# A block product without sums taken second, in a bank of its own, in the last two tiles of an attention + GELU feed-forward kernel

## The chip, the cores and the metric

The kernel runs on one NeuronCore of a Trainium2 chip. The metric is the device time of one execution in microseconds. A core has five engines with instruction queues of their own, each worked off in order: TensorE (PE in the profile, its weight loads PEld), VectorE (DVE), ScalarE (ACT), GpSimd (POOL) and SyncE (SP), which here only issues DMAs. TensorE writes to PSUM, a memory of eight banks that hold 512 fp32 numbers in each of 128 partitions; VectorE and ScalarE read the results from there.

## The reference

Sliding-window attention over 8 batches and 8 heads (576 positions, 64 channels, a window of 32 to each side), followed by a feed-forward layer on all 4608 tokens:

```python
scores = (q @ k^T) / 8, masked to |i - j| <= 32
attn   = softmax(scores);  o = attn @ v
x = o.transpose(0, 2, 1, 3).reshape(4608, 512)
h = x @ w_in                                            # 512 -> 2048
g = 0.5 * h * (1 + tanh(sqrt(2/pi) * (h + 0.044715 * h**3)))
out = g @ w_out                                         # 2048 -> 512, fp32
```

All inputs and the output are fp32; the kernel multiplies in fp16 and sums in fp32.

## The kernel before

The 4608 tokens are worked on in nine tiles of 512 (t = 0 to 8). One pass of the main loop (line 911) brings the feed-forward of tile t and, woven into it, the attention of a later batch. ffn_in makes the transposed hidden values in PSUM, gelu (on ScalarE) puts them into the fp16 tile gT, and ffn_out multiplies them with w_out16.

From tile 1 on the second layer is a Winograd-Strassen product of 2x2 blocks: seven block products in place of eight. gT is cut into blocks A11, A12, A21, A22 (halves of the hidden columns and of the tokens), w_out16 into B11 to B22, and VectorE makes sums of the gelus, S1 to S4 (sums, line 672, instructions of L680), as these come. T1 to T4 are differences of the weights, made once. The table WINO (line 41) names the seven products in the order in which they are taken, each with a flag that says whether it begins a new sum in its bank:

| n | product | bank | what is read from the bank after it |
|---|---|---|---|
| 0 | A11*B11 | pys[0], new | M1 = copy (ScalarE in tiles 7 and 8, L748), kept where C21 will be |
| 1 | S2*T2 | pys[1], new | U2 = bank + M1 (L750), kept in C12 |
| 2 | A12*B21 | pys[0], on top of n = 0 | C11 = copy (L752) |
| 3 | S3*T3 | pys[1], on top of n = 1 | U3 = bank + M1 (L757), kept in C22 |
| 4 | S1*T1 | pys[0], new | C22 = bank + U3 (L760; in tile 8 two halves, L763) |
| 5 | A22*T4 | pys[1], on top of n = 3 | C21 = bank + M1 (L766), then stores of rows 2 and 3 |
| 6 | S4*B22 | pys[0], on top of n = 4 | C12 = bank + U2 in two halves (ffn_last, L775), then stores of rows 0 and 1 |

"Rows" are the four groups of 128 tokens of a tile, held in yo. Each product is 16 matmuls of 128x128 weights and 256 columns: eight hidden blocks f for each of two token groups blk. The loop index i runs over the 112 matmuls, so n = i // 16. In the last two tiles product 1 takes six blocks f of both token groups first and the last two of both afterwards. Matmuls and evacuations are put into the queues in this order; a dependence between engines becomes a semaphore wait on the later instruction. A product that goes on in a bank can start only when what was read from the bank before has been read.

In tiles 7 and 8 the first layer is a Winograd product too. in_mixed (line 618) goes through the list MIX (line 62), an order of products, copies, gelus and sums written by hand. It ends `g14 15 gA01 gB01 t1 t2 g15 t3 u1 u2 u3`: gelus of plain columns (L643) and of combined ones (L639), and the sums S1, S2 (t) and S3, S4 (u) of gelu columns 1 to 3.

In tile 7 the pass of ffn_out also holds the end of the last batch's attention: at i = 40 its value products (v-1, L481 and L491), at i = 66 the division (x-1, L532), and at i = 84 in_x (line 592, L600), four VectorE subtractions that prepare tile 8's first layer. Tile 8 has nothing beside its products. Its second token group in n = 4 and n = 6 goes to a bank of its own (pys["apart"], tile py in the profile), so that C22 and C12 can be read in halves. Tile 7 stores through GpSimd's queue (four or five DMAs a store of two rows), tile 8 through SyncE's and ScalarE's (L697 and L699).

psS holds two tiles of two banks, with the tags S0 and S1. In tiles 7 and 8 S1 is used by in_mixed for the third product of the first layer (pu2) and is then unused until the next tile.

Of the kernel before, what the change touches and what calls it, by code (L numbers as in the profile page):

```python
# [9 lines left out]
FP32 = mybir.dt.float32  # L10
FP16 = mybir.dt.float16
AF = mybir.ActivationFunctionType
ALU = mybir.AluOpType
# [23 lines left out]
def cut(b):  # L37
    return 120 if b else 128
# [23 lines left out]
MIX = ("3 g3 A0 s0A B0 s0B A2 B2 cA00 cB00 A1 s1A A4 B1 s1B gA00 gB00 B4 t0 u0 12 A3 s3A B3 s3B g12 cA11 cB11 13 "  # L62
       "A5 B5 gA11 gB11 g13 14 gA10 gB10 A6 B6 cA01 cB01 g14 15 gA01 gB01 t1 t2 g15 t3 u1 u2 u3").split()
UNITS = {"A": 1, "B": 2}

PLAN_1 = {12: "s0@0 s1@1 s2", 16: "m0 m1", 36: "m2", 45: "v0@1 v1 s-1@0", 52: "x0", 55: "x1", 62: "m-1",
          69: "s3@0 v2 v-1@1", 73: "m3", 81: "x2", 85: "x-1", 91: "v3 s4@1", 112: "x3 m4"}
# [11 lines left out]
def kernel(  # L79
# [9 lines left out]
    nc = tc.nc  # L89
# [5 lines left out]
    NT = NTOK // 512  # L95
# [22 lines left out]
    psS = ctx.enter_context(tc.tile_pool(name="psS", bufs=1, space=PSUM))  # L118
# [229 lines left out]
    def bank(i):  # L348

        return psM.tile([128, 512], FP32, name="mm", tag=f"x{i}")  # L350
# [158 lines left out]
    def size(b, g):  # L509
        return 4 * cut(b) if g < 4 else 4 * NPAIR * (144 - cut(b))  # L510
# [66 lines left out]
    def in_w(eng, unit, *which):  # L577

        i = UNITS[unit]
        A11, A12, A21, A22 = (w_in16[:, d:d + 2, c + 256 * i:c + 256 * i + 256] for c in (0, 1024) for d in (0, 2))  # L580
# [21 lines left out]
    def in_product(unit, n):  # L602
        a, w, new = WINO[n]
        if n == 0:
            phs[unit, "a"] = psO.tile([128, 512], FP32, name="pu", tag="O") if unit == "A" else bank(1)
        elif n in (2, 4):
            which = "b" if n == 2 else "c"
            if unit == "A":
                phs[which] = psS.tile([128, 2, 512], FP32, name="pu2", tag="S1" if n == 2 else "S0")
            phs[unit, which] = phs[which][:, "AB".index(unit), :]  # L610
        ps = phs[unit, "b" if n == 2 else "c" if n in (4, 6) else "a"]
        lhs, rhs = mixed[unit, "w"][a], mixed["x"][w]
        for h in range(2):
            for d in range(2):
                nc.tensor.matmul(ps[:, 256 * h:256 * h + 256], lhs[:, d, 128 * h:128 * h + 128], rhs[:, d, :],  # L615
                                 start=(n in (0, 2, 4) and h == d == 0), stop=(h == d == 1), skip_group_check=True)

    def in_mixed(t):
# [5 lines left out]
        for step in MIX:  # L624
            kind, rest = step[0], step[1:]
            if kind in UNITS:
                in_product(kind, int(rest))
# [4 lines left out]
            elif kind == "c":  # L632
                x, which = place[rest[1:]]
                x = mixed[rest[0]][:, x, :]
                nc.vector.tensor_tensor(x, phs[rest[0], which], x, op=ALU.add)
            elif kind == "g" and rest[0] in UNITS:
                r, c, j = int(rest[1]), int(rest[2]), UNITS[rest[0]]
                src = phs[rest[0], "a"] if rest[1:] == "10" else mixed[rest[0]][:, place[rest[1:]][0], :]
# [44 lines left out]
    pys = {}  # L683

    def store(t, t4, yo, cols=slice(0, 512), *engs):

        m = i = 0
        while m < 128:
            b, c = divmod(t * 512 + t4 * 128 + m, S)
            q0, n = (0, cut(b)) if c < 4 * cut(b) else (cut(b), 144 - cut(b))  # L690
            j, p = divmod(c - 4 * q0, n)
            e = min(n - p, 128 - m)
            nj = 1 if p else max(1, min(4 - j, (128 - m) // n))
            eng = engs[i % len(engs)] if engs else nc.gpsimd
            if nj > 1:
                e = nj * n
                eng.dma_start(out_v[b, j:j + nj, q0:q0 + n, cols], yo[m:m + e, cols])  # L697
            else:
                eng.dma_start(out_v[b, j, q0 + p:q0 + p + e, cols], yo[m:m + e, cols])  # L699
            m += e  # L700
            i += 1
# [16 lines left out]
    def ffn_out(t, i):  # L718

        n, blk, f = i // 16, i // 8 % 2, i % 8  # L720
        if n == 1 and t >= NT - 2:
            blk, f = divmod(i % 16, 6) if i % 16 < 12 else (i // 2 % 2, 6 + i % 2)
        a, w, new = WINO[n]
        end = t == NT - 1
        if i % 16 == 0 and new:
            pys[n % 2] = bank((1 + n) % 2)
            if end and n == 4:
                pys["apart"] = psO.tile([128, 512], FP32, name="py2", tag="O")
        py = pys[n % 2].rearrange("p (b c) -> p b c", b=2)
        apart = end and blk and n in (4, 6)  # L730
        if a[0] == "A":
            r0, c0 = 8 * (int(a[2]) - 1) + f, 256 * (int(a[1]) - 1) + 128 * blk
            lhsT = gTs[t][:, r0, c0:c0 + 128]
        else:
            lhsT = wino[a][:, f, 128 * blk:128 * blk + 128]
        one = end and n in (4, 6)
        nc.tensor.matmul(pys["apart"][:, 0:256] if apart else py[:, blk, :], lhsT,  # L737
                         wino[w][:, f, :], start=(new and i % (8 if one else 16) == 0),
                         stop=(i % (8 if one else 16) == (7 if one else 15)),
                         skip_group_check=True)  # L740
        if i % 16 < 15:
            return
        yo, left, right = wino["yo"], slice(0, 256), slice(256, 512)
        C11, C12, C21, C22 = (yo[:, r:r + 2, c] for r in (0, 2) for c in (left, right))

        M1, U2, U3 = C21, C12, C22
        if n == 0:
            (nc.scalar.copy if t >= NT - 2 else nc.vector.tensor_copy)(M1, py)  # L748
        elif n == 1:
            nc.vector.tensor_tensor(U2, py, M1, op=ALU.add)  # L750
        elif n == 2:
            nc.vector.tensor_copy(C11, py)  # L752
            if end:
                for x in range(2):
                    store(t, x, yo[:, x, :], left, nc.sync)
        elif n == 3:
            nc.vector.tensor_tensor(U3, py, M1, op=ALU.add)  # L757
        elif n == 4:
            if not end:
                nc.vector.tensor_tensor(C22, py, U3, op=ALU.add)  # L760
            else:
                for x, part in enumerate((py[:, 0, :], pys["apart"][:, 0:256])):
                    nc.vector.tensor_tensor(C22[:, x, :], part, U3[:, x, :], op=ALU.add)  # L763
                    store(t, 2 + x, yo[:, 2 + x, :], right, nc.sync, nc.scalar)
        elif n == 5:
            nc.vector.tensor_tensor(C21, py, M1, op=ALU.add)  # L766
            for x in range(2):
                store(t, 2 + x, yo[:, 2 + x, :], *((left, nc.sync, nc.scalar) if end else ()))

    def ffn_last(t):  # L770
        py = pys[0].rearrange("p (b c) -> p b c", b=2)
# [139 lines left out]
    for t in range(NT):  # L911
        b = t + 1
# [37 lines left out]
        for i in range(113 if t else 65):  # L950
# [5 lines left out]
            for act in plan.get(i, "").split():  # L956
# [18 lines left out]
                elif kind in "np":  # L975
# [7 lines left out]
                    if kind == "n":  # L983
                        n = size(1, g)
# [45 lines left out]
            if t == 0 and i < 64:  # L1030
                ffn_out_0(*ORDER_0[i])
            elif t and i < 112:
                ffn_out(t, i)
# [36 lines left out]
```

## Time and profile before

| | |
|---|---|
| time, median of 5 runs | 302.72 us (301.56 to 305.35) |
| the profiled execution's own time | 303.57 us |
| its span, first to last instruction | 301.9 us |
| mean granted TensorE clock | 0.999 |
| TensorE busy | 286.7 us, 95% of the span |
| VectorE, ScalarE, GpSimd busy | 212.3, 195.2, 99.6 us |
| tile 7's second layer: first matmul of n = 0, first of n = 6 | 257.45 us, 269.04 us |
| tile 8's second layer: first matmul of n = 0, first of n = 6 | 283.96 us, 295.32 us |
| last addition of tile 8 | 297.26 to 297.68 us |

The page of the profile gives busy times, waits and chains of waits by source line. Lines of the instructions in order of time read: start in us, length in us, engine, source line, operation, output <- input (a buffer's name without its number), partitions x columns and type, how often, and in brackets the idle time of that engine just before and what ended it. In the names mm is a bank of pys or of the first layer, s one of the sums S1 to S4, t one of T1 to T4, w_out one of the blocks B, y the output tile yo, and xc the values of in_x. A matmul's length includes the time in which its last results drain, so the distance between the starts is what it costs in a stream.

### The profile page before, as it was taken

The page shows a single profiled execution, that of the slowest core. Times are in us where ns is not written, and L with a number is a line of the kernel's source. Part 1 is how long each engine was busy: PE and PEld are TensorE (multiplying, and loading weights), DVE is VectorE, ACT ScalarE, POOL GpSimd, SP SyncE. Part 2 cuts the span into 40 slices and gives each one's busy share as a digit, 9 for nine tenths or more (in the row PEclk, how much of TensorE's full clock was granted, in tenths as well). Part 3 has the DMA queues.
Part 4 walks back from the last instruction along what each step waited for, and adds up shares of the span by engine and source line. Part 5 has one row for each costly group of instructions (what it writes and reads, how often), then busy time and mean ns, then how long its engine had stood idle before and what let it go on. Part 6 is the DMA issues. An engine that isn't in the chain of part 4 may idle for free.

```text
span 301.9 us, 7286 instructions
## 1 busy us (share of the span) xinstructions
PE 286.7 (95%) x2941; PEld 183.8 (61%) x2941; DVE 212.3 (70%) x467; ACT 195.2 (65%) x313; POOL 99.6 (33%) x149
## 2 busy tenths in 40 slices
PE   7899899899999799999999799999999999999993
PEld 2534444446774488458845685478647867786683
DVE  4752577897975875868586968766896677865772
ACT  4866667679667676578657846686668656715700
POOL 3435425302843070507280906050720070015000
PEclk9999999999999999999999999999999999999999
DMA  7999998999999999898998995989691031004013
GB/s 216 269 294 383 355 289 235 251 198 180 238 186 186 173 247 208 154 144 215 171 198 125 244 141 127 138 211 177 119 192 31 2 82 62 2 3 137 1 39 103
DMA packets 115944, 50.76 MB, mean 168 GB/s; under 512 B 97495, under 2 KB 109399, under 8 KB 115910
## 3 DMA queue, kind: packets, MB, share of 16 engines
q1 hardware_dynamic: 86756, 37.62, 60.3%
q0 software_dynamic: 28032, 11.62, 26.6%
q10 hardware_dynamic: 1122, 1.06, 1.1%
q8 instruction: 23, 0.38, 0.6%
q14 instruction: 11, 0.09, 0.1%
HBM read 36.70 MB, written 9.44 MB: 153 GB/s over the span
## 4 chain that ended last, share of the span: by engine, by line
PE 60%; DMA 19%; SPq 7%; ACT 5%; DVE 5%; issue 2%; POOL 0%; DVEq 0%; ACTq 0%
PE mm L737 26%; PE mm L563 12%; PE ph L563 12%; DMA wst<-in_moe_w_in_dram 5%; DMA kr<-in_k_dram 4%; DMA tr<-in_q_dram 4%; DMA KT<-k 3%; PE ps_s L454 2%; PE pu L615 2%; PE ps_d L481 2%; DMA wst<-in_moe_w_out_dram 2%; DVE s L680 2%; SPq L182 2%; ACT gT L639 2%; DMA tr<-in_k_dram 2%
## 5 line engine op out<-in xcount | busy, mean ns | idle before, releaser
L563 PEld LDWEIGHTS <-w_in 128*128 128x128 f16 x512 | 49.6, 98 | 57.2 <-DVE w_in L228 0.8
L563 PE MATMUL ph<-xT,w_in 128*128 128x512 f16 x256 | 64.1, 379 | 0.2 <-POOL w_in L853 0.2
L563 PE MATMUL mm<-xT,w_in 128*128 128x512 f16 x256 | 63.7, 379 | 0.0
L571 ACT ACTIVATE gT<-mm 128x512 f16<-128x512 f32 x60 | 35.6, 597 | 33.3 <-PE mm L563 32.7
L737 PEld LDWEIGHTS <-s 128*128 128x128 f16 x512 | 49.4, 98 | 7.6 <-issue 0.9
L699 POOL DMA_DIRECT2D out_dram<-y x55 | 32.4, 597 | 59.4 <-DVE y L766 45.6
L737 PE MATMUL mm<-t,s 128*128 128x256 f16 x376 | 45.0, 273 | 0.6 <-DVE y L750 0.2
L737 PEld LDWEIGHTS <-gT 128*128 128x128 f16 x384 | 36.0, 98 | 6.9 <-issue 0.5
L467 ACT ACTIVATE pe<-ps_s 128x960 f16<-128x960 f32 (+1 forms) x31 | 29.5, 975 | 15.8 <-PE ps_s L454 15.7
L571 ACT ACTIVATE gT<-ph 128x512 f16<-128x512 f32 x58 | 32.2, 600 | 11.1 <-PE ph L563 11.1
L680 DVE TENSOR_TENSOR s<-gT 128x512 f16<-128x512 f16 x64 | 26.7, 418 | 15.6 <-ACT gT L571 14.5
L737 PE MATMUL mm<-w_out,gT 128*128 128x256 f16 x256 | 32.8, 273 | 0.0
L104 ACT ACT_TABLE_LOAD x18 | 23.1, 1283 | 2.2 <-issue 1.9
L516 ACT ACTIVATE lt<-ps_d 128x480 f32<-128x480 f32 (+2 forms) x28 | 15.6, 556 | 11.3 <-PE ps_d L481 7.7
L517 ACT ACTIVATE lt<-lt 128x480 f32<-128x480 f32 (+3 forms) x36 | 21.1, 586 | 1.1
L476 DVE TENSOR_TENSOR pe<-pe,band 128x960 f16<-128x960 f16 x28 | 20.8, 758 | 1.1 <-ACT pe L467 0.9
L194 POOL DMA_DIRECT2D V<-in_v_dram x20 | 17.9, 909 | 1.4 <-issue 1.4
L491 PEld LDWEIGHTS <-V 128*64 128x64 f16 x520 | 13.9, 111 | 6.4 <-DVE V L204 1.5
L737 PE MATMUL mm<-t,gT 128*128 128x256 f16 x128 | 16.3, 273 | 0.0
L680 DVE TENSOR_TENSOR s<-s,gT 128x512 f16<-128x512 f16 x32 | 15.2, 474 | 1.1
L454 PE MATMUL ps_s<-QT,KT 64*64 64x128 f16 (+3 forms) x576 | 13.5, 216 | 2.5 <-DMA KT<-k 1.8
L454 PEld LDWEIGHTS <-KT 64*64 64x64 f16 x576 | 10.0, 106 | 8.6 <-issue 3.8
(148 smaller groups left out, 396.6 us busy)
## 6 DMA issues: line engine op xcount, KB each, us to landing
kr<-in_k_dram SPq DMA_DIRECT2D x31, 256.0 KB, 11.1
qr<-in_q_dram SPq DMA_DIRECT2D x6, 1024.0 KB
wst<-in_moe_w_in_dram SPq DMA_DIRECT2D x7, 512.0 KB, 8.1
V<-in_v_dram POOLq DMA_DIRECT2D x20, 128.0 KB, 8.6
wst<-in_moe_w_out_dram SPq DMA_DIRECT2D x2, 1024.0 KB
wst<-in_moe_w_out_dram SPq DMA_DIRECT2D x4, 512.0 KB
qr<-in_q_dram SPq DMA_DIRECT2D x7, 256.0 KB, 8.3
out_dram<-y POOLq DMA_DIRECT2D x6, 192.0 KB, 5.8
```

Of the source, the lines that this page charges most:

```text
L104: nc.scalar.add_instruction(mybir.InstLoadActFuncSet(name=nc.get_next_instruction_name(), act_func_set_id=which, ins=[], outs=[]))
L194: nc.gpsimd.dma_start(V[:, c, :, :], v[b, :, 128 * c:128 * c + 128, :].rearrange("h p d -> p h d"))
L454: nc.tensor.matmul(sides[h][64 * half:64 * half + 64, 4 * n * r:4 * n * r + 4 * n].rearrange("k (j p) -> k j p", j=4)[:, :, p0 - q0:p1 - q ...
L467: nc.scalar.activation(pe, ps[:, :, 0:w], AF.Exp, scale=SCALE)
L476: nc.vector.tensor_tensor(pe, pe, m.rearrange("k (o j) p -> k o j p", o=1).broadcast_to(list(pe.shape)), op=ALU.mult)
L516: nc.scalar.activation(lt[:, 0:n], d[:, 0:n], AF.Ln)
L517: nc.scalar.activation(lt[:, 0:n], lt[:, 0:n], AF.Exp, scale=-1.0)
L563: nc.tensor.matmul(ph, w_in16[:, dc, fc * 128:fc * 128 + 128], xT[:, dc, t * 512 % RING:t * 512 % RING + 512], start=(dc == 0), stop=(dc = ...
L571: nc.scalar.activation(gTs[t][:, fc, :], phs[fc], AF.Gelu_apprx_tanh)
L680: nc.vector.tensor_tensor(dst, x, y, op=op)
L699: eng.dma_start(out_v[b, j, q0 + p:q0 + p + e, cols], yo[m:m + e, cols])
L737: nc.tensor.matmul(pys["apart"][:, 0:256] if apart else py[:, blk, :], lhsT, wino[w][:, f, :], start=(new and i % (8 if one else 16) == 0) ...
```

## The change

In tiles 7 and 8 the seven products are taken in the order 0, 5, 1, 2, 3, 4, 6. Product 5 (A22*T4), which needs no sums of gelus, comes second. It begins a sum of its own in the first bank of S1 (py5) instead of going on in pys[1]. C21 is then this bank plus U3, added by VectorE right behind U3 and thus behind product 3. U3 holds the other two products of C21 and M1, so the value is the same. The stores of rows 2 and 3 follow C22 in tile 7; in tile 8 the left columns are stored behind C21 and the right columns behind C22. Product 1 takes its blocks in the plain order, all of one token group and then all of the other. Tiles 1 to 6 are as before.

```diff
+ORDER = [0, 5, 1, 2, 3, 4, 6]
...
     def ffn_out(t, i):
 
         n, blk, f = i // 16, i // 8 % 2, i % 8
-        if n == 1 and t >= NT - 2:
-            blk, f = divmod(i % 16, 6) if i % 16 < 12 else (i // 2 % 2, 6 + i % 2)
+        late = t >= NT - 2
+        if late:
+            n = ORDER[n]
         a, w, new = WINO[n]
         end = t == NT - 1
-        if i % 16 == 0 and new:
+        if late and n == 5:
+            new = True
+            if i % 16 == 0:
+                pys["apart5"] = psS.tile([128, 2, 512], FP32, name="py5", tag="S1")[:, 0, :]
+        elif i % 16 == 0 and new:
             pys[n % 2] = bank((1 + n) % 2)
             if end and n == 4:
                 pys["apart"] = psO.tile([128, 512], FP32, name="py2", tag="O")
-        py = pys[n % 2].rearrange("p (b c) -> p b c", b=2)
+        py, py5 = (pys[x].rearrange("p (b c) -> p b c", b=2) if x in pys else None
+                   for x in ("apart5" if late and n == 5 else n % 2, "apart5"))
         apart = end and blk and n in (4, 6)
...
         elif n == 3:
             nc.vector.tensor_tensor(U3, py, M1, op=ALU.add)
+            if late:
+                nc.vector.tensor_tensor(C21, py5, U3, op=ALU.add)
+                if end:
+                    for x in range(2):
+                        store(t, 2 + x, yo[:, 2 + x, :], left, nc.sync, nc.scalar)
         elif n == 4:
             if not end:
                 nc.vector.tensor_tensor(C22, py, U3, op=ALU.add)
+                if late:
+                    for x in range(2):
+                        store(t, 2 + x, yo[:, 2 + x, :])
             else:
                 for x, part in enumerate((py[:, 0, :], pys["apart"][:, 0:256])):
                     nc.vector.tensor_tensor(C22[:, x, :], part, U3[:, x, :], op=ALU.add)
                     store(t, 2 + x, yo[:, 2 + x, :], right, nc.sync, nc.scalar)
-        elif n == 5:
+        elif n == 5 and not late:
             nc.vector.tensor_tensor(C21, py, M1, op=ALU.add)
             for x in range(2):
-                store(t, 2 + x, yo[:, 2 + x, :], *((left, nc.sync, nc.scalar) if end else ()))
+                store(t, 2 + x, yo[:, 2 + x, :])
```

## The prediction

> **What bounds the kernel now.** I read the page first, for the bounding engine, then the chain of work that ended last from 250 us on, and then the instructions in order of time, engine by engine, in tiles 7 and 8, the only ones that the change touches. The page:
>
> ```profile
> span 301.9 us, 7286 instructions
> PE 286.7 (95%) x2941; PEld 183.8 (61%) x2941; DVE 212.3 (70%) x467; ACT 195.2 (65%) x313; POOL 99.6 (33%) x149
> ```
>
> TensorE is the bound overall. In late tiles, the little time that it doesn't work is what the change can win. The chain shows where the end hangs on something else (start, length, what):
>
> ```profile
> 259.69 0.43 DVE s L680
> 260.12 0.05 issue
> 260.17 2.36 PE mm L737 x20
> ...
> 289.42 0.61 DVE y L750
> 290.04 0.04 issue
> 290.08 2.78 PE mm L737 x24
> ```
>
> In tile 7 the second product (S2*T2) is held by VectorE's sums of gelus (L680). In tile 8 the fourth is held by the add L750, which itself stands behind the sums in VectorE's queue. Tile 7 in order of time:
>
> ```profile
> 257.45 1.91 PE L737 MATMUL mm<-w_out,gT 128*128 128x256 f16 x16
> 258.79 0.62 ACT L643 ACTIVATE gT<-mm 128x512 f16<-128x512 f32 x1
> 259.46 2.19 PE L737 MATMUL mm<-t,s 128*128 128x256 f16 x16
> 260.17 1.21 PEld L737 LDWEIGHTS <-s 128*128 128x128 f16 x12 [0.39 <-DVE s L680]
> ```
>
> The 32 unbroken matmuls from 263.80 to the next product at 267.29 give 109 ns each, **1.745 us a product** (a group's length adds the last one's drain). So product 0 leaves TensorE free at 259.20. Product 1 starts at 259.46: its bank is the last plain gelu's, read until 258.79+0.62 = 259.41. Four matmuls later (259.90) it waits for the sums until 260.17. **Two holes, 0.26 + 0.27 = 0.53 us.** Tile 8 has the same two (start 285.97, then 286.68), and a third, 0.34 us: product 2 ends at 288.00+1.745 = 289.74, product 3 starts at 290.08. There is no such hole in tile 7, where attention matmuls take 0.55 us in product 2 (262.36 to 262.91).
>
> What VectorE has to do at the end of tile 7:
>
> ```profile
> 265.74 0.69 DVE L757 TENSOR_TENSOR y<-mm,y 128x512 f32<-128x512 f32 x1 [1.05 <-PE mm L737]
> 267.49 0.69 DVE L760 TENSOR_TENSOR y<-mm,y 128x512 f32<-128x512 f32 x1 [0.59 <-PE mm L737]
> 268.10 0.41 DVE L600 TENSOR_TENSOR xc<-xT 128x512 f16<-128x512 f16 x1
> 268.55 0.42 DVE L600 TENSOR_TENSOR xc<-xT,xc 128x512 f16<-128x512 f16 x1
> ...
> 269.56 0.68 DVE L766 TENSOR_TENSOR y<-mm,y 128x512 f32<-128x512 f32 x1
> ```
>
> L760 is C22, which reads the bank in which product 6 later goes on. Today product 5 (267.29 to 269.04) covers it. The four L600 subtractions for tile 8 stand behind it, 1.46 us from the first's start to L766's.
>
> **What the skill says.** The Trainium skill, PSUM — Partial Sum Buffer, section PSUM bank collisions raise a hardware error: the chip doesn't arbitrate when TensorE writes a bank that VectorE reads, so such accesses must be ordered by a semaphore. The trace agrees: L750 ends at 290.02, and product 3, into the bank it read, starts at 290.08. Perfetto Trace Analysis, section Matmuls (under Optimizing Tensor Performance), wants independent groups to rotate through banks, so that one's evacuation lies under the next one's matmuls. The old order 4, 5, 6 does that; 4, 6 doesn't. TensorE: Matmul & The Clock Gate, section What's actually happening: TensorE falls to half clock after an idle window of about 3.4 us. Here it never waits so long late in the span, and the granted clock is 1.00 in every stage of both tiles.
>
> **The change, part by part.** No work is added: 112 product matmuls and seven evacuations by VectorE or ScalarE in each tile (eight or nine in tile 8, where some are halved), before and after. Product 5 moves from sixth to second; its add moves from behind product 5 to behind U3, and reads U3 instead of M1, in the same shape (L766, 0.69 us).
>
> *Second place (gain).* Product 5 needs gelus and a bank unused since early in the tile, no sums. It runs 259.20 to 260.94. Its eighth weight is the row of the gelu that ends at 259.41, and it is wanted at about 259.9: no wait, 0.5 us to spare. Product 1 then starts at 260.94, when its bank (259.41) is free; its last sums are the sixth of the L680 operations, from 260.48 to 260.90, and wanted 0.65 us after its start. Tile 7 wins **0.53**. In tile 8 product 1 runs 287.45 to 289.20, product 2 to 290.94. L750 still waits for the sums to get out of VectorE's way, runs 289.40 to 290.08, and product 2 covers it. Tile 8 wins 0.53 + 0.34 = **0.87**. The dropped interleaving of the two halves of product 1 costs nothing under this cover; uncovered it would put the sums' wait back, at most 0.5 a tile.
>
> *Product 6 right behind 4 in tile 7 (loss).* New times: products 0, 5, 1 and the attention end at 263.24, 2 at 264.98, 3 at 266.73, 4 at 268.47. VectorE's queue then has, in program order, U3 (L757), C21, the four L600 (still issued at i = 84, now inside product 4) and C22 (L760's operation). U3 starts 0.20 behind product 3, as before (265.74 against 265.54): 266.93. C21 reads U3, so it starts at its end and 0.04: 267.66 (independent ones follow in 0.61, dependent L680 ones at end + 0.03). L600 starts 0.61 later, 268.27, C22 1.46 after that, 269.73, and ends at 270.42. With 0.05 for the release product 6 starts at **270.47**, a wait of 2.00 us behind product 4. Before, it started at 269.04. Net for tile 7: 2.00 - 0.53 = +1.47, or by the two starts **+1.43**; I use this. Queued behind the waiting matmul is all of TensorE: product 6 and the first matmuls of tile 8. From there the order is the old one, so tile 8 is late by the whole of it. Bounds: below, only C22 itself if the L600 are out of its way (0.20+0.69+0.05 = 0.94 of wait, net +0.4); above, +1.9 if the whole queue is 0.5 later. The attention's division (266.35, 0.55) is no part of it: issued at i = 66, now ahead of U3, and under product 3. The stores of rows 2 and 3 on POOL's queue are issued behind C22 instead of C21, still just before product 6; POOL is idle there (22 us before its first store).
>
> *The same place in tile 8.* Here C22 is two halves, the second in a bank of its own, so product 6's first half needs only the first half of C22. Product 4's first half ends at 293.56. VectorE: U3 292.89, C21 293.62, first C22 half 0.61 later, 294.23 to 294.65. Product 4 ends at 294.43, product 6 starts at 294.70: a wait of 0.27. The second half of C22 (from 294.63, 0.42) ends under it. Product 6 ends at 296.44 instead of 297.06: tile 8 nets **-0.62** (0.87 - 0.27, rounded starts).
>
> *The end.* The last add is at 297.06 instead of 297.68, plus tile 7's delay. Behind it the span ran 4.2 us more. C21's left stores (SP and ACT queues, two each) are issued behind C21, and so ahead of C22's; before they stood just ahead of the last ones. ACT's six issues take 0.33 to 0.75 each; four of them now run from 294.35 to about 296.7, and the last two up to about 297.5: level with the last add. SP has four C11 issues (2.6 us, from about 291.9 now instead of 290.66) and six of about 0.33: free in time. The data are 768 KB behind C21 and C22 and the last adds; the three slices from 297 to 300 moved 169, 158 and 195 GB/s, at 174 that is 4.4 us from about 294.8: 299.2, just when the last stores would land anyway. I take **+0.1**, bounds 0 and +0.5.
>
> Sum: 1.43 - 0.62 + 0.1 = **+0.9 us** against the profiled execution's 303.57 (span 301.9, and 1.7 around it): 304.5. That execution lies 0.85 above the median of the runs, so I give 302.72 + 0.9 = **303.6**.
>
> **The rivals.**
> *Cover stays (10%).* The L600 don't delay C22, because the scheduler of dependences or other data hold them back or let them go first: wait 0.94, sum 0.4 - 0.62 + 0.1 = -0.1, 302.6. Against it: VectorE takes its queue in order, and the L600 started the moment L760 let them.
> *No wait at 6 at all (8%).* Gains alone: -0.53 - 0.87 + 0.27 + 0.1 = -1.0, 301.7. The 0.06 us release at 290.08 speaks against it.
> *The early product gains nothing (10%):* product 5 is held by its last gelu row or its bank as long as product 1 was, so the holes stay. 0.9 + 0.53 + 0.87 = +2.3, 305.0. The gelu's end at 259.41 speaks against it.
> *Slower: the clock (5%).* The new hole in product 6 of tile 7 makes TensorE fall to half clock for two of the skill's windows, 2 x 3.4 us at half rate, 3.4 us lost: 0.9 + 3.4 = +4.3, 307.0. It decides from an idle stretch of a whole window; mine is 2.0, and the longest wait of TensorE in the old trace for which a releaser is named is 1.8 us (a key transpose), with the mean clock at 0.999.
> *Stores at the end jam (5%),* at half the rate seen: 768 KB at 87 GB/s is 8.8 us, 4.4 more, 308.0.
>
> **How the numbers follow.** Forecast 62%: 303.6, own range 303.1 to 304.6 by the bounds. Range 301.9 to 305.2: it takes in the rivals at 302.6 and 305.0, and leaves out no-wait and the two slow ones (18%). Medians of five that lie between 301.56 and 305.35 can also move by about 1 us. What a measurement can tell is about 1%, 3.0 us: within it lie all but the two slow cases. Same 86%, slower 11% (the two, and noise on the third), faster 3% (noise below no-wait).
>
> **What would show it.** In both tiles the 16 matmuls on w_out and gT of product 0 run unbroken into 16 on t and gT, and no wait of TensorE or its weight loads for L680 is left in either tile. A wait of TensorE for C22's add appears ahead of the w_out,s matmuls of tile 7, about 2 us, with the four L600 ahead of that add, and about 0.3 in tile 8. The gap from the last add to the end stays near 4.2. I am wrong if L600 starts before C21, if product 5 waits, or if the last store is issued more than 0.5 us after the last add.

## The result, and the profile after

The changed kernel takes 1.0037 times the time of before (95% interval 1.0019 to 1.0055): about +1.1 us, between 0.6 and 1.7. The medians of all runs are 303.88 us after and 303.54 before. The forecast was +0.9. This is well within the 1% that I had named as "no change", but with this many runs it is a small, real loss. The profiled execution of the changed kernel took 304.66 us, with a span of 302.9, 1.0 more than before.

Its page:

```profile
span 302.9 us, 7285 instructions
PE 287.1 (95%) x2941; PEld 184.6 (61%) x2941; DVE 213.5 (70%) x467; ACT 195.3 (64%) x313; POOL 100.1 (33%) x149
```

The same work, then, with nearly the same engine times (VectorE has 1.2 us more, TensorE 0.4). The chain that ended last, where it leads to product 6 of tile 7 and of tile 8 (start, length, what):

```profile
262.34 4.49 PE mm L745 x40
266.83 0.02 issue
266.85 0.70 DVE y L765
...
268.63 1.09 DVE xc L602 x3
269.73 0.61 DVE y L773
270.34 0.04 issue
270.38 1.91 PE mm L745 x16
...
288.95 5.25 PE mm L745 x48
294.20 0.02 issue
294.23 0.70 DVE y L765
294.93 0.02 issue
294.95 0.70 DVE y L767
...
295.75 0.44 DVE y L779
296.18 0.04 issue
296.23 1.03 PE mm L745 x8
```

Before, the chain went through the sums (L680 then, L682 now) and through U2 (L750, now L758) ahead of products 1 and 3. Neither is in it any more: up to product 3 both tiles are matmuls end to end. In their place are the adds behind product 3, U3 (L765), C21 (L767), in tile 7 in_x (L602), and C22 (L773, in halves L779). They end at product 6.

Tile 7 of the changed kernel in order of time:

```profile
257.36 1.91 PE L745 MATMUL mm<-w_out,gT 128*128 128x256 f16 x16
259.10 1.91 PE L745 MATMUL py<-t,gT 128*128 128x256 f16 x16
260.85 1.04 PE L745 MATMUL mm<-t,s 128*128 128x256 f16 x8
...
267.57 0.69 DVE L767 TENSOR_TENSOR y<-py,y 128x512 f32<-128x512 f32 x1
268.18 0.41 DVE L602 TENSOR_TENSOR xc<-xT 128x512 f16<-128x512 f16 x1
...
269.65 0.68 DVE L773 TENSOR_TENSOR y<-mm,y 128x512 f32<-128x512 f32 x1
270.38 1.91 PE L745 MATMUL mm<-w_out,s 128*128 128x256 f16 x16 [1.82 <-DVE y L773]
```

Products 0, 5 and 1 start 1.74 and 1.75 us apart, without a hole. Products 3 and 4 start at 264.90, so 4 ends at 268.39; product 6 starts at 270.38. That is a wait of 1.99 us (the 1.82 in brackets leave out the drain of the last matmul).

Between executions, the tiles ahead of tile 7 differ by several us (product 0 of tile 7 starts between 253.7 and 261.6 us in the fourteen kernels here). So I compare stages that begin there. Executions that lie over 1.5% above the fastest of their kernel are left out of the ratios, not of the medians, and the profiles of in_x_twice, order_43_26 and last_on_pool are of such executions, so that their spans can't be compared with the others. In this table, each column is the difference of two starts or ends from the instructions in order of time, in us; "tail" runs from the end of the last add to the end of the span. From product 6 of tile 7 to product 0 of tile 8 all fourteen take 14.91 to 14.93.

| kernel | tile 7: product 0 to 6 | tile 8: product 0 to 6 | tile 8: product 0 to last add | tail | time ratio to before (95%) |
|---|---|---|---|---|---|
| before | 11.59 | 11.36 | 13.72 | 4.22 | 1 |
| after | 13.02 | 10.93 | 13.29 | 4.31 | 1.0037 (1.0019 to 1.0055) |
| t7_only | 13.02 | 11.37 | 13.73 | 5.09 | 1.0057 (1.0027 to 1.0088) |
| t8_only | 11.59 | 10.93 | 13.30 | 4.25 | 0.9978 (0.9950 to 1.0006) |
| in_x_behind | 11.98 | 10.93 | 13.30 | 4.81 | 0.9976 (0.9946 to 1.0005) |
| in_x_twice | 14.49 | 10.93 | 13.29 | 4.49 | 1.0109 (1.0002 to 1.0217) |
| own_bank_6 | 11.03 | 10.93 | 13.29 | 4.31 | 0.9958 (0.9930 to 0.9985) |
| u3_elsewhere | 13.03 | 10.74 | 13.10 | 4.81 | one run |
| own_bank_6_both | 11.04 | 10.48 | 12.85 | 5.14 | 0.9984 (0.9956 to 1.0011) |
| order_43_26 | 11.55 | 11.07 | 13.43 | 8.84 | 1.0169 (1.0096 to 1.0241) |
| order_43_26_pool | 11.03 | 10.48 | 12.85 | 9.30 | 1.0160 (1.0110 to 1.0210) |
| last_on_pool | 13.02 | 10.93 | 13.29 | 5.67 | 1.0118 (1.0063 to 1.0174) |
| split_96 | 13.02 | 10.93 | 13.29 | 4.27 | 1.0055 (1.0027 to 1.0083) |
| own_6_split_96 | 11.04 | 10.48 | 12.84 | 4.75 | 0.9988 (0.9961 to 1.0015) |

The whole change in these stages: +1.43 in tile 7, -0.43 in tile 8 up to the last add, +0.09 in the tail, 1.09 in sum. The span grew by 1.0 since tile 7 began 0.09 earlier.

### The profile page after: what moved, and what is told of

It is laid out like the page before. It is cut to its first block, busy times and chain, and to the rows that moved or that the text cites. A ratio compares the mean times of both kernels' runs of the same rounds, so it can differ in the third digit from the quotient of the medians.

```text
span 302.9 us, 7285 instructions
## 1 busy us (share of the span) xinstructions
PE 287.1 (95%) x2941; PEld 184.6 (61%) x2941; DVE 213.5 (70%) x467; ACT 195.3 (64%) x313; POOL 100.1 (33%) x149
## 4 chain that ended last, share of the span: by engine, by line
PE 66%; DMA 19%; DVE 5%; SPq 5%; issue 2%; POOL 1%; ACT 0%; DVEq 0%
PE mm L745 28%; PE mm L565 13%; PE ph L565 12%; DMA wst<-in_moe_w_in_dram 5%; DMA tr<-in_q_dram 4%; DMA kr<-in_k_dram 3%; DMA KT<-k 3%; PE pu L617 3%; PE ps_s L456 3%; DMA wst<-in_moe_w_out_dram 2%; PE ps_d L483 2%; DMA qr<-in_v_dram 2%; PE ps_o L493 2%; SPq L242 2%; PE py L745 1%
## 5 line engine op out<-in xcount | busy, mean ns | idle before, releaser
L682 DVE TENSOR_TENSOR s<-gT 128x512 f16<-128x512 f16 x64 | 26.7, 417 | 14.3 <-ACT gT L573 13.3
L745 PE MATMUL mm<-w_out,s 128*128 128x256 f16 x120 | 14.4, 272 | 2.1 <-DVE y L773 1.8
L968 POOL COPY after<-KL 128x1 f16<-128x1 f16 x5 | 1.7, 334 | 43.9 <-DMA KL<-kt 43.9
L682 DVE TENSOR_TENSOR s<-s,gT 128x512 f16<-128x512 f16 x32 | 15.2, 474 | 1.1
```

The source lines that it names most:

```text
L682: nc.vector.tensor_tensor(dst, x, y, op=op)
```

## The experiments

All are edits of the changed kernel. The theory is the prediction's: the early product removes the holes, and product 6 of tile 7 then waits for C22, which stands in VectorE's queue behind U3, C21 and in_x.

### One tile alone

t7_only has the new order in tile 7 only, t8_only in tile 8 only:

```diff
-        late = t >= NT - 2
+        late = t == NT - 2        # t8_only: NT - 1
         if late:
             n = ORDER[n]
+        elif n == 1 and t >= NT - 2:
+            blk, f = divmod(i % 16, 6) if i % 16 < 12 else (i // 2 % 2, 6 + i % 2)
```

(and the old stores behind product 5 where tile 8 has the old order).

> The new order in tile 7 alone, the old one in tile 8. Theory (product 6 waits for C22, which stands in VectorE's queue behind U3, C21 and the four L600): the first matmul of product 6 starts 13.0 us after that of product 0 in tile 7, as in the changed kernel (11.6 before); span and time +1.4 us over before, more than the whole change (+1.0 by the spans). Rival 'late stores' (the cost comes from the stores pressed together at the end of tile 8): the time is that of before, within 0.3 us.

> The new order in tile 8 alone, the old one in tile 7. Theory: tile 8 takes 0.43 us less from product 0 to the last add, the stores at the end give back 0.1, so the time is 0.3 us under before. Rival 'late stores': the time is 0.5 us or more over before, with a longer stretch from the last add to the end of the span. Rival 'the early product gains nothing': the holes of 0.53 and 0.34 us in tile 8 are still there, the time is that of before or 0.4 over.

Measured: tile 7 alone costs 13.02 - 11.59 = 1.43 us, in time +1.7 (0.8 to 2.7). Tile 8 alone wins 0.42 us up to the last add, in time -0.7 (-1.5 to +0.2). With the old tile 8, and so the old stores at the end, the loss is there in full. The rival "late stores" falls for this change. "The early product gains nothing" falls by the stage: its holes are gone; by the time alone, whose interval takes in no gain, it wouldn't.

### What stands ahead of C22

in_x_behind moves the four subtractions behind C22, in_x_twice does them twice ahead of it:

```diff
-            if t == NT - 2 and i == 84:
+            if t == NT - 2 and i == 96:        # in_x_behind
                 in_x(t + 1)
```

```diff
             if t == NT - 2 and i == 84:
                 in_x(t + 1)
+                in_x(t + 1, again=True)        # in_x_twice: the same values into the same tile
```

> The changed kernel, with the four L600 subtractions of in_x put behind C22 in VectorE's queue (issued at i = 96 instead of 84). Theory: C22 starts 0.2 us behind product 4 instead of 1.26, product 6's wait falls from 1.99 to 0.94 us, the time by 1.05 us against the changed kernel, so it is level with before (within 0.2). Rival 'C22 alone' (the wait is the price of the order 4, 6 and has nothing to do with L600): the wait stays at 2.0, the time 1.0 us over before.

> The changed kernel, with the four L600 of tile 7 done twice (the same values again), so that eight of them stand ahead of C22. Theory: 1.46 us more ahead of C22, product 6's wait grows from 1.99 to 3.45 us, the time by 1.46 against the changed kernel, 2.5 us over before; the granted clock stays at full. Rival 'the clock': an idle stretch as long as that lets TensorE fall to half clock, and the matmuls behind it start 0.22 instead of 0.11 us apart for some 3.4 us; another 1.7 us or more, at least 4.2 over before. Rival 'C22 alone': no more than the changed kernel.

Two lines of in_x_behind, C22's add and the product behind it, and then the same two of in_x_twice:

```profile
264.93 0.69 DVE L773 TENSOR_TENSOR y<-mm,y 128x512 f32<-128x512 f32 x1 [0.33 <-PE mm L745]
...
265.67 1.91 PE L745 MATMUL mm<-w_out,s 128*128 128x256 f16 x16 [0.78 <-DVE y L773]
```

```profile
272.86 0.68 DVE L773 TENSOR_TENSOR y<-mm,y 128x512 f32<-128x512 f32 x1
...
273.60 1.91 PE L745 MATMUL mm<-w_out,s 128*128 128x256 f16 x16 [3.29 <-DVE y L773]
```

In the first, VectorE had been idle for 0.33 us and C22 waited for product 4 itself: what is left, 11.98 - 11.03 = 0.95 us, is the price of the order 4, 6 with none of in_x ahead of C22. In the second, the stage is 1.47 us longer than in the changed kernel, by the four operations more. So about half of the 1.99 us is C22 itself and half in_x. The times agree: -0.7 us against before (-1.6 to +0.2), and +3.3 (0.1 to 6.6, of few runs). The rival "C22 alone" falls. So does "the clock", as far as one profiled execution can tell: the hole is 3.46 us long, no shorter than the 3.4 us that this rival names, the granted clock is 1.00 in it and behind it, and product 6 to product 0 of tile 8 takes the same 14.92 us.

### A bank of its own for product 6

own_bank_6 gives product 6 of tile 7 the second bank of the tile in which product 5 has the first. VectorE adds product 4's bank to U2 ahead of the last add:

```diff
-                pys["apart5"] = psS.tile([128, 2, 512], FP32, name="py5", tag="S1")[:, 0, :]
+                both = psS.tile([128, 2, 512], FP32, name="py5", tag="S1")
+                pys["apart5"], pys["own6"] = both[:, 0, :], both[:, 1, :]
+        elif t == NT - 2 and n == 6:
+            new = True
...
                 nc.vector.tensor_tensor(C22, py, U3, op=ALU.add)
                 if late:
+                    nc.vector.tensor_tensor(U2, py, U2, op=ALU.add)
...
     def ffn_last(t):
-        py = pys[0].rearrange("p (b c) -> p b c", b=2)
+        py = pys["own6" if t == NT - 2 else 0].rearrange("p (b c) -> p b c", b=2)
```

> The changed kernel, with product 6 of tile 7 in the second bank of S1 instead of on top of product 4; VectorE adds product 4's bank to U2 first (one add of 0.69 us more, under product 6). Theory: nothing of product 6 waits for C22, it starts right behind product 4 (11.0 us after product 0), and the time falls by 2.0 us against the changed kernel to 1.0 us under before. Rival 'C22 alone' gives the same here. Rival 'late stores': no more than 0.3 us of change against the changed kernel.

Product 4, what stands ahead of C22, and product 6 in own_bank_6:

```profile
263.83 1.91 PE L748 MATMUL mm<-t,s 128*128 128x256 f16 x16
...
265.36 0.42 DVE L602 TENSOR_TENSOR xc<-xT 128x512 f16<-128x512 f16 x1
265.57 1.91 PE L748 MATMUL py<-w_out,s 128*128 128x256 f16 x16
...
266.83 0.69 DVE L776 TENSOR_TENSOR y<-mm,y 128x512 f32<-128x512 f32 x1
```

Product 6 starts 1.74 us after product 4, while VectorE is still at in_x and C22 (L776) comes 1.26 us later. The wait is gone, 1.99 us, and **this kernel beats both**: 0.9958 of before (0.9930 to 0.9985), -1.3 us (-2.1 to -0.5). So what product 6 of tile 7 waited for was its bank, until C22 had read it. Of the 0.9 us that the table's stages and tail give for this kernel, 0.56 are the holes of tile 7 and 0.43 the gain of tile 8, less 0.09 in the tail.

own_bank_6_both does the same in tile 8, where the second half of product 6 goes to bank(0) (late instead of t == NT - 2 in the edit above, and the two adds to U2 in halves).

> The changed kernel, with product 6 in a bank of its own in both tiles (in tile 8 its second half goes to the bank of pys[1], which is free by then), and product 4's bank added to U2 first. Theory: no wait of product 6 in either tile: 11.0 us from product 0 to 6 in tile 7, 10.5 in tile 8, stores as in the changed kernel. That is 2.0 + 0.46 us less than the changed kernel, about 1.4 under before. Rival 'the early product gains nothing': no less than before.

Its products run as expected (11.04 and 10.48). But the forecast of the time is missed: 0.9984 (0.9956 to 1.0011) is -0.5 us (-1.3 to +0.3), not -1.4. It can't be told from own_bank_6 by these intervals, and what the last product gained, 0.44 us up to the last add, does not show in the time. In its one profile the tail is 0.83 us longer than in own_bank_6 (5.14 for 4.31); why is not shown.

### Why product 6 of tile 8 waited longer than forecast

The prediction had 0.27 us there; the changed kernel has 0.46 (product 4's 32 matmuls with 3 from 292.28 end at 295.77, product 6 starts at 296.23). C22's first half starts 0.80 us after C21 instead of 0.61. It overwrites U3, which C21 reads, and so it has to wait until C21 has ended. u3_elsewhere takes that dependence away:

```diff
         M1, U2, U3 = C21, C12, C22
+        if late:
+            U3 = mixed["A"][:, 0, :].rearrange("p (r c) -> p r c", r=2)
```

> The changed kernel, with U3 kept in a spare tile instead of in C22's place, so that C22's add in tile 8 doesn't overwrite what C21's add reads. Theory: the first half of C22 in tile 8 starts 0.61 us after C21's start instead of 0.80, and product 6's wait behind product 4 falls from 0.46 to about 0.27 us, as the prediction had it. Rival 'the separate wait instruction': the 0.80 stay.

C21, the first half of C22 and product 6 in it:

```profile
295.35 0.69 DVE L769 TENSOR_TENSOR y<-py,sa 128x512 f32<-128x512 f32 x1
295.96 0.41 DVE L781 TENSOR_TENSOR y<-mm,sa 128x256 f32<-128x256 f32 x1
...
296.43 1.03 PE L745 MATMUL mm<-w_out,s 128*128 128x256 f16 x8
```

0.61 us, and a stage of 10.74 instead of 10.93: the term is found. The separate wait instruction of VectorE ahead of C22 is gone in this kernel too (in the changed one it takes 0.02 us), so the run doesn't tell the wait for C21's end from that instruction; both come with the dependence.

### An order without the wait, and what the end does to it

order_43_26 puts product 2 between 3 and 6, to cover C22, with product 4 and 6 in a bank of their own. Its stores in tile 8 differ too: rows 2 and 3 go out at full width behind C21 (the two largest of these stores move 192 and 176 KB), and C11 over SP and ACT in turn. The first lines of the edit:

```diff
-ORDER = [0, 5, 1, 2, 3, 4, 6]
+ORDER = [0, 5, 1, 4, 3, 2, 6]
...
```

> A version that should beat both: order 0, 5, 1, 4, 3, 2, 6 in tiles 7 and 8, product 4 in the second bank of S1 (product 6 goes on there), U3 in a spare tile, C22 added ahead of C21 right behind U3, so that product 2 covers what product 6 waits for. Theory: the seven products of both tiles run without a hole (11.0 us from product 0 to product 6 in tile 7, 10.5 in tile 8), which is 0.53 and 0.87 us less than before; the stores at the end, now C11's just before the last ones, give back 0.1 to 0.3. 1.1 to 1.3 us under before, 2.2 under the changed kernel. Rival 'C22 alone': the same. Rival 'late stores': level with before.

It is a clear miss: 1.0169 (1.0096 to 1.0241), +5.1 us for a forecast of -1.1 to -1.3. Two things went wrong. Product 6 still waited some 0.5 us in each tile, for C21's add: it reads the other half of the tile that product 6 writes. And the tail grew to 8.84 us. All four row groups, 1 MB, become due for storing between 297.27 and 299.66 here, and the rival "late stores", dead for the change itself, was right in kind for this kernel, though not in size (it said level with before). Its last store was issued only at 305.71. In the program's lists of waits it waits until the store eight places before on SP's and ACT's common count, the 192 KB of 96 rows issued at 297.91, has landed. The next run mends the first and tries a cause of the second:

```diff
-                both = psS.tile([128, 2, 512], FP32, name="py5", tag="S1")
-                pys["apart5"], pys["four"] = both[:, 0, :], both[:, 1, :]
+                pys["apart5"], pys["four"] = (psS.tile([128, 2, 512], FP32, name=f"py{x}", tag=f"S{x % 2 ^ 1}")[:, 0, :] for x in (5, 4))
...
-                    store(t, 2 + x, yo[:, 2 + x, :], *((slice(0, 512), nc.sync, nc.scalar) if end else ()))
+                    store(t, 2 + x, yo[:, 2 + x, :], slice(0, 512))
```

> The order 0, 5, 1, 4, 3, 2, 6 again, with two edits. Product 5's bank lies in S0, apart from product 4's in S1 (in order_43_26 product 6 waited 0.5 us for C21's add, which reads the other half of the same tile), and rows 2 and 3 of tile 8 go out through GpSimd's queue. Theory A (in order_43_26 the end was late by 4.6 us because each store of SP and ACT waits until the one eight places before it has landed, and 192 KB took 6.8 us to land): with only eight stores left on SP and ACT the last one is issued within 0.5 us of the last add, 4.5 to 5.5 us lie between it and the end, no product waits, and the time is 0.5 to 1.4 us under before. Theory B (the DMA engines themselves can't move 1 MB in the last 4 us): 7 us or more from the last add to the end, 1.5 us or more over before.

The products now run without a hole (11.03 and 10.48), so the wait for C21's add is found. The tail is 9.30 us and the time 1.0160 (1.0110 to 1.0210), +4.8 us: theory A falls, and what theory B forecast came out. Engine times of order_43_26_pool by stage (columns: stage, its length, PE, PEld, DVE, ACT, POOL busy with counts, clock, DMA share, GB/s):

```profile
299.00:300.00 1.00, 0.00 (x0) 0.00 (x0) 0.00 (x0) 0.00 (x0) 0.60 (x1) 1.00 0.83 225
300.00:301.00 1.00, 0.00 (x0) 0.00 (x0) 0.00 (x0) 0.00 (x0) 0.00 (x0) 0.86 1.04 248
...
302.00:303.00 1.00, 0.00 (x0) 0.00 (x0) 0.00 (x0) 0.00 (x0) 0.00 (x0) 0.50 0.69 137
303.00:304.00 1.00, 0.00 (x0) 0.00 (x0) 0.00 (x0) 0.00 (x0) 0.00 (x0) 0.50 0.20 71
304.00:305.00 1.00, 0.00 (x0) 0.00 (x0) 0.00 (x0) 0.00 (x0) 0.00 (x0) 0.50 0.20 82
305.00:306.00 1.00, 0.00 (x0) 0.00 (x0) 0.00 (x0) 0.00 (x0) 0.00 (x0) 0.50 0.02 8
```

The last store is issued by 299.6 (POOL's 0.60 us in the first line). So the wait for a place isn't needed to make this end late. Theory B is only a part of it, though. Until 303 the DMA engines are busy, and move about 0.89 of 1.05 MB. Then the rest trickles at a DMA share of 0.20 until 305.4, and from there nothing moves until the span ends at 308.2. The trickle may be the store of 96 rows in four groups of 24, 192 KB: issued at 298.89, it landed 6.8 us later, while the 176 KB of 88 rows, issued 1 us before it, took 4.5. (The 6.8 us that the expectation gives for it in order_43_26 was misread: it is an 80-row store's there. The 192 KB held the last store of that kernel for 7.8 us.) And the quiet end is longer with GpSimd: 2.8 us here and 2.6 in last_on_pool, the two kernels in which it stores rows of tile 8, but 1.5 to 1.8 us in the other twelve. No run took these parts of the tail apart in this order.

### The tail of the changed kernel

Here a step of the prediction did fail: the changed kernel's last store goes out late.

```profile
299.66 0.33 ACTq L701 DMA_DIRECT2D out_dram<-y  x1
```

That is 1.07 us behind the end of the last add (298.59); before, it was 0.21 (297.89 and 297.68). In the program's lists of waits, a store on SP or ACT waits until the one eight places before has landed, and here that is the first 96-row store, issued at 296.33, 3.33 us earlier. In the six other kernels that have the new order 0, 5, 1, 2, 3, 4, 6 in tile 8 and these stores, the last one goes out 3.1 to 3.3 us behind that store too. Two edits tried the end, one of them also on own_bank_6_both:

```diff
-                store(t, x, yo[:, x, :], right, nc.sync, nc.scalar)
+                store(t, x, yo[:, x, :], right, nc.sync, nc.gpsimd if x else nc.scalar)        # last_on_pool
```

```diff
-            nj = 1 if p else max(1, min(4 - j, (128 - m) // n))
+            nj = 1 if p or (engs and n == 24) else max(1, min(4 - j, (128 - m) // n))        # split_96
```

> The changed kernel, with its very last store (80 rows of tile 8) issued on GpSimd's queue instead of ACT's. In the changed kernel ACT issues it 1.1 us behind the last add. Theory A (it waits there for an earlier store's landing): GpSimd issues it within 0.2 us of the last add, and the end comes 0.3 to 0.8 us sooner after the last add than the 4.3 us of the changed kernel. Theory B (the data of the earlier stores hold it anyway): 4.3 us as before.

> The changed kernel, with the 96-row stores of tile 8 (4 groups of 24 rows in one DMA) issued as four stores of 24 rows each, by SP and ACT in turn. Theory (the 96-row DMA lands slowly, 192 KB of it took 6.8 us, and the stores that reuse its semaphore wait for it): the last store is issued 0.1 to 0.6 us behind the last add instead of 1.1, and the end comes 0.3 to 1.0 us sooner after it than the 4.3 us of the changed kernel; the matmuls stay where they are. Rival 'issue': six more DMAs on queues that are busy make the stretch from last add to end 4.5 us or more.

> own_bank_6_both with the same split of the 96-row stores. Its products run without a hole, but 5.1 us lay between its last add and the end, 0.8 more than in the changed kernel. Theory (the 96-row store sets that end): 3.8 to 4.3 us, and the time is 1.0 to 1.8 us under before. Rival 'issue': 5 us or more, the time within 0.5 us of before.

In last_on_pool the tail is 5.67 us: GpSimd issues the store only 0.30 us behind the add (302.83), but the end comes later, not sooner. The last two stores:

```profile
303.13 0.56 POOL L701 DMA_DIRECT2D out_dram<-y  x1 [22.85 <-DVE y L791]
303.86 0.31 SPq L701 DMA_DIRECT2D out_dram<-y  x1
```

With ACT's last store gone, SP's last one has the place eight behind the 96-row store. It goes out 1.03 us behind the add (0.03 in the changed kernel), and 3.28 us behind that store. So the store does wait for an earlier one's landing, as theory A has it. But the edit handed this wait on instead of removing it, and so what its removal would do to the end was not put to the test. Data move until 3.1 us behind the add, 2.8 in the changed kernel; most of the longer tail is the longer quiet end, 2.6 us for 1.5. The time ratio of 1.0118, of three runs, agrees with a tail longer by 1.4 us, which would make 1.0082.

In split_96 the last store goes out 1.42 us behind the add, not 0.1 to 0.6, and the tail is 4.27. In own_6_split_96 these are 1.86 and 4.75, between the theory's tail and the rival's. The last issue alone doesn't set the end: 0.21, 1.07 and 1.42 us behind the add (before, after, split_96) go with tails of 4.22, 4.31 and 4.27. With the old tile 8 the tail was 4.22 in one kernel and 5.09 in another, so one profile of each can't tell tails that differ by less than about 0.9 us, and the two splits show no gain (1.0055 and 0.9988, for 1.0037 and 0.9984 without them). Whether the 96-row store sets the end of the changed kernel stays open.

## Why the prediction was right

**The holes.** Forecast: 0.53 us gone in tile 7, 0.87 in tile 8, since product 5 needs no sums and covers them. Measured: no hole in the first six products of either tile, and product 1 started 3.49 us after product 0, as forecast. own_bank_6_both, without a wait at product 6, shows the gains alone: 0.55 and 0.88.

**Product 6 in tile 7.** Forecast 2.00 us of wait, 13.02 from product 0 to 6; measured 1.99 and 13.02. The working, a queue read off the old trace and put in a new order, held to 0.01 us, and so did each step of it: from the start of product 0, U3 began at 9.49 (9.48 forecast), C21 at 10.21 (10.21), in_x at 10.82 (10.82), C22 at 12.29 (12.28). Edits took the wait apart: C22 without in_x 0.95 (forecast 0.94), and in_x 1.04, or 1.47 for four more of its operations, since C22 without in_x still waits for product 4.

**Product 6 in tile 8.** Forecast -0.62, measured -0.43. This is nearly all of the distance between the forecast's +0.9 and the 1.09 of the stages. The mis-sized term is "first C22 half 0.61 later": C22 overwrites what C21 reads, so it starts at C21's end and 0.11, at 0.80. u3_elsewhere gives the forecast's 10.74.

**The end.** Forecast +0.1, measured +0.09, but not for the reasons given. The last store was not "level with the last add"; the condition that I had set for being wrong, 0.5 us, was passed (1.07). That the number fits is luck: tails of one and the same tile 8 differ by up to 0.9 us, so this term was not shown either way.

**The rivals.** "Cover stays" is what in_x_behind makes of the change, and it was not the change itself. "No wait at 6 at all" has a sum that keeps the 0.27 us of tile 8, so it is a forecast for own_bank_6: -1.0, where the stages give -0.9. "The clock" fell with in_x_twice. Late stores do occur, but in another order than the changed one, with stores of other shapes.

## What to carry to other kernels

When a step is moved out of a sequence, look at what it was covering: product 5 hid the read of a bank between two products that share it, and in tile 7 the cover that it took away was worth 1.99 us, more than the 0.56 us of waits that it removed at its new place. In tile 8, with C22 in halves and no other work in VectorE's queue, it was the other way round: 0.46 lost for 0.88 won. Write the queue of the engine that frees the bank in its new order, with all that is queued ahead (here work for the next tile), and the wait can come out to a hundredth of a microsecond, as in tile 7. Look then for what each operation overwrites, too: that was the term missed in tile 8. A bank of its own for product 6 of tile 7, and one more add under cover, kept the gain without the wait. At the end of a kernel, a product that is done sooner isn't yet a sooner end: the 0.44 us won there did not show in the time, for a reason that stays open.

## What the runs showed of the hardware

- A VectorE add that overwrites what the add before it reads started 0.11 us after that one's end, with a separate wait instruction between them; an independent one starts 0.08 us before it (0.69 long, 0.61 from start to start).
- A TensorE wait of 3.46 us in in_x_twice cost nothing beyond itself: the granted clock stayed 1.00, and the next stage took 14.92 us as in the kernels without it. This is one execution.
- In order_43_26_pool one DMA of 192 KB from 96 partitions to four groups of 24 rows took 6.8 us to land, and 176 KB from 88 partitions in one group 4.5 us, issued 1 us apart on the same queue, among other stores.
- In the two kernels in which GpSimd issued stores of tile 8, order_43_26_pool and last_on_pool, 2.8 and 2.6 us lay between the last data moved and the end of the span; in the other twelve it was 1.5 to 1.8 us.
- In the changed kernel and six others the last store went out 3.1 to 3.3 us behind the store eight places before it on SP's and ACT's common count, which was 0.9 to 1.5 us behind the last add.
